# Key and value casts one step ahead, and a new order for the opening steps, in a retention and feed-forward kernel on one core

## The chip, the core and the metric

The kernel runs on one core of a Trainium2 chip. A core has a matrix engine (TensorE, PE in the profile; its weight loads are listed as PEld), a vector engine (VectorE, DVE), a scalar engine (ScalarE, ACT), GpSimd (POOL) and SyncE (SP), which here issues all transfers. Each engine works through a list of instructions of its own; semaphores tie the lists together. The metric is the time of one launch in microseconds, the median of several runs. Lower is better.

## What is computed

```python
gamma = 1.0 - 2.0 ** (-5.0 - np.arange(H, dtype=np.float32))
scale = 1.0 / np.sqrt(D)
for t in range(S):
    state = gamma[None, :, None, None] * state + np.einsum('bhd,bhe->bhde', k[:, :, t], v[:, :, t])
    y[:, :, t] = scale * np.einsum('bhd,bhde->bhe', q[:, :, t], state)
...
x = np.ascontiguousarray(attn_out.transpose(0, 2, 1, 3)).reshape(B * S, H * D)
...
a = x @ w1
b = x @ w2
h = a * b @ w3
return (h @ w_out).astype(np.float32)
```

Batch 4, 8 heads, 768 positions, head size 64; w1 and w2 are 512 x 1024, w3 is 1024 x 1024, w_out 1024 x 512. All inputs and the output (3072 x 512) are float32.

## The kernel before

w3 and w_out are multiplied first into one matrix (W3O), so each block of rows needs three products: with w1, with w2, and, after their elementwise product, with W3O. Operands are cast to 16 bits on the way in.

The recurrence is worked in chunks of 128 positions, two batch elements at a time: 6 chunks for 2 pairs of batch elements make 12 steps, m = 0 to 11. A chunk is split into two halves of 64 positions. For a step m the parts are:

- `load_k`, `load_v`, `load_q`: transfers from HBM into staging tiles (22 buffers of 512 KB, `wstage`), all issued by SP in the order of the calls. `load_q(n)` covers two chunks of one batch element, so two of them serve two steps.
- `q_cast`, `k_cast` (L269, L283): casts to 16 bits, on GpSimd or ScalarE; `v_cast` (L290): cast with the decay factors, on GpSimd.
- The transposes of queries and keys: in the opening on TensorE (`q_transposes`, `k_transposes`, L302 and L330, with copies back from PSUM by VectorE or ScalarE), later by transfers that SP issues (`q_dma` L313, `k_dma` L335).
- `scores` (L358) and their masking on VectorE (L365); `intra` (L380), the part of the output within a half; `kv` (L400), the new term of the state, with its backs on VectorE (L414, L417) and GpSimd (L418); `inter` (L431), the part of the output from the state; `outputs_back` (L440), which makes the rows x for the feed-forward part.
- The feed-forward part `Ffn(m)`: eight A units (four matmuls L460 into one of four psF banks, copied out by ScalarE, L469), eight B units (four matmuls L460, multiplied with A on VectorE, L475), and two output units (eight matmuls L485, scaled by ScalarE, L489, written out by SP, L490).

The order on each engine is the order of the calls in the source[...]. One call of `step(m)` does `inter` of step m-1, `scores` of step m, the two output units of step m-2, then the A and B units of step m-1 with `intra` and `kv` of step m in between. It also runs the preparation: keys, values and queries are loaded about three steps ahead and cast about two steps ahead (`k_cast(m + 2)` stands between the A units, `q_cast(m + 4)` at the end of GpSimd's list).

The opening is written out by hand: weights of W3O first, then the queries, keys and values of step 0, w1, keys and values 1, w2, and so on. The feed-forward part of step 0 goes by rows of w1 and w2 (`by_rows`, L570) so that each weight tile is used as it arrives; its W1 results are parked in two staging tiles (`hold`). `busy(n)` (L503) issues n matmuls on zeros. A few lines that set the order in the loop:

```python
if m > 2:
    q_dma(m + 3)
    load_k(m + 3)
    ffn[m - 2].o_unit(0)
    load_v(m + 3)
    ffn[m - 2].o_unit(1)
    load_q(m + 5)
...
elif m + 2 < NSTEP:
    k_cast(m + 2, (nc.scalar,))
    v_cast(m + 2, (nc.gpsimd, nc.gpsimd))
q_cast(m + 4, nc.gpsimd)
```

Of the kernel before, what the change touches and what calls it, by code (L numbers as in the profile page):

```python
# [18 lines left out]
def kernel(  # L19
# [11 lines left out]
    nc = tc.nc  # L31
# [5 lines left out]
    NSTEP = (B // 2) * NCH  # L37
# [4 lines left out]
    K_PE = 4  # L42
# [23 lines left out]
    def load_q(n):  # L66

        g, e = divmod(n, 2)
        if g >= NSTEP // 2:
            return  # L70
        bp, cp = divmod(g, NCH // 2)
        t = new_stage()
        dma_in(
            t[:, :].rearrange("p (h x) -> p h x", x=2 * D),
            q[bp * 2 + e, :, cp * 2 * C : (cp + 1) * 2 * C, :].rearrange("h (p t) d -> p h (t d)", t=2),
        )
        q_in[n] = t

    def load_k(m):
        load_kv(m, k_in, k)  # L80

    def load_v(m):
        load_kv(m, v_in, v)
# [41 lines left out]
    w3_st = {f: load_rows(moe_w3, f) for f in range(4, 8)}  # L125
    load_q(0)
    load_q(1)
    load_k(0)
    load_v(0)
    w1_st = [load_rows(moe_w1, d) for d in range(4)]  # L130
    load_k(1)
    load_v(1)
    w2_st = [load_rows(moe_w2, d) for d in range(4)]
    load_q(2)
    load_q(3)
    for m in range(2, 5):
        load_k(m)
        load_v(m)
        load_q(m + 2)

    Z = const.tile([128, 512], HP, name="zeros")
    nc.vector.memset(Z[:, :].bitcast(FP), 0.0)  # L142
# [42 lines left out]
    W1 = [wpool.tile([128, DFF], HP, name=f"w1_{i}") for i in range(4)]  # L185
# [6 lines left out]
    def cast_to(dst, src, on_dve):  # L192
        if on_dve:
            nc.vector.tensor_copy(dst, src)
        else:
            nc.scalar.copy(dst, src)  # L196
# [78 lines left out]
    def k_cast(m, engs):  # L275
        k16 = att.tile([128, 2, 512], HP, tag="k16", name="k16", bufs=3)
        k32 = k_in.pop(m)
        if len(engs) == 1:
            parts = [(k16[:, :, :].rearrange("p e x -> p (e x)"), k32[:, :, :].rearrange("p e x -> p (e x)"))]
        else:  # L280
            parts = [(k16[:, e, :], k32[:, e, :]) for e in range(2)]
        for eng, (dst, src) in zip(engs, parts):
            (nc.scalar.copy if eng is nc.scalar else eng.tensor_copy)(dst, src)  # L283
        k16s[m] = k16
# [37 lines left out]
    def k_transposes(m, tag, on_dve):  # L322
        k16, kT = k16s[m], new_kT(m)
        if tag:
            ps = bank(tag, [128, 2, NP, 128], HP, "psTk")
        else:
            ps = ps_f.tile([128, 2, NP, 128], HP, tag="psF", name="psTk")
        for e in range(2):
            for p in range(NP):
                nc.tensor.transpose(ps[:, e, p, :], k16[:, e, p * 128 : (p + 1) * 128], ident16[:, :])  # L330
        for e in range(2):
            cast_to(kT[:, e, :, :], ps[:, e, :, :], on_dve[e])
# [17 lines left out]
    def scores(m, engs=None):  # L350
        kT = kTs.pop(m)
        am = att.tile([128, 2, NP * 2, L], HP, tag="am", name="am")
        ps = [bank(f"X{r}", [128, NP * 2, L], FP, "psA") for r in range(2)]
        for e in range(2):
            for p in range(NP):
                for r in range(2):
                    for s in range(2):
                        nc.tensor.matmul(  # L358
                            ps[r][half(s), p * 2 + e, :], lhsT=kT[half(r), e, p, half(s)],
                            rhs=queries(m, e, p, s, r), start=True, stop=True,  # L360
                        )
        AMs[m] = am

        def back(r):
            nc.vector.tensor_tensor(  # L365
                am[:, r, :, :], ps[r][:, :, :],
                keep[:, :].unsqueeze(1).broadcast_to((128, NP * 2, L)), MULT,
            )

        return back  # L370
# [52 lines left out]
    def inter(m):  # L423
        ps = psYs[m]
        t = [Ts[m, s] for s in range(2)]
        first = t[0] is None
        for e in range(2):
            for p in range(NP):
                u = p * 2 + e
                for s, r in ((1, 0), (1, 1)) if first else ((1, 0), (0, 1), (0, 0), (1, 1)):  # L430
                    nc.tensor.matmul(  # L431
                        ps[s][half(r), u, :], lhsT=t[s][half(r), u * L : (u + 1) * L],
                        rhs=queries(m, e, p, s, r), start=False, stop=(e == 1 and p == NP - 1),
                    )
# [62 lines left out]
    def cast_w(W, st, d, on_dve):  # L497
        cast_to(W[d][:, :], st[d][:, :], on_dve)

    def busy(m, tag="Y0"):  # L500
        ps = bank(tag, [128, 512], FP, "psZ")
        for _ in range(m):
            nc.tensor.matmul(ps[:, :], lhsT=Z[:, 0:128], rhs=Z[:, 0:512], start=True, stop=True)  # L503
# [30 lines left out]
    k_transposes(0, "X0", (True, False))  # L534
    w3o_back()
    v_cast(0, (nc.gpsimd, nc.vector))
    nc.gpsimd.tensor_copy(W1[1][:, :], w1_st[1][:, :])
    cast_w(W1, w1_st, 0, False)
    backs = []

    def first_scores():
        backs.append(scores(0))

    w3o_back = w3_mm(7, first_scores)
    w3o_back()
    backs[0](0)
    backs[0](1)
    intra(0)
    backs.append(kv(0, True))
    busy(3, "X0")  # L550
    backs[1](0)
    inter(0)
    busy(3, "X1")
    outputs_back(0, 0)
    outputs_back(0, 1)
    backs[1](1)
    cast_w(W1, w1_st, 2, False)
    cast_w(W1, w1_st, 3, False)

    ffn = [Ffn(m) for m in range(NSTEP)]  # L560
    f0, f1 = ffn[0], ffn[1]
# [3 lines left out]
    def four_banks():  # L565
        return [ps_f.tile([128, 2, TB], FP, tag="psF", name="psF")[:, :, :] for _ in range(4)]

    def by_rows(W, ps, d, blocks=range(8)):
        for f in blocks:
            nc.tensor.matmul(  # L570
                ps[f // 2][:, f % 2, :], lhsT=W[d][:, f * 128 : (f + 1) * 128],
                rhs=f0.x(d), start=(d == 0 and f % 2 == 0), stop=(d == 3 and f % 2 == 1),
            )

    k_cast(1, (nc.gpsimd, nc.scalar))
    ps = four_banks()
    by_rows(W1, ps, 0)
    by_rows(W1, ps, 1)
    by_rows(W1, ps, 2)
    k_transposes(1, "Y0", (True, False))  # L580
    by_rows(W1, ps, 3, range(4))
    pa = [hold[i // 2][:, i % 2 * 512 : i % 2 * 512 + 512].rearrange("p (a n) -> p a n", a=2) for i in range(4)]
    am_back = scores(1)
    by_rows(W1, ps, 3, range(4, 8))
    for i in range(4):
        cast_to(pa[i], ps[i], False)
    am_back(0)
    am_back(1)
    v_cast(1, (nc.gpsimd, nc.gpsimd))
    nc.gpsimd.tensor_copy(W2[0][:, :], w2_st[0][:, :])  # L590
    ps = four_banks()
    cast_w(W2, w2_st, 1, False)
    intra(1)
    kv_back = kv(1)
    kv_back(0, nc.vector)
    by_rows(W2, ps, 0)
    inter(1)
    outputs_back(1, 1)
    outputs_back(1, 0)
    cast_w(W2, w2_st, 2, False)  # L600
    nc.gpsimd.tensor_copy(W2[3][:, 512:1024], w2_st[3][:, 512:1024])
    q_cast(2, nc.gpsimd)
    kv_back(1)
    by_rows(W2, ps, 1)
    nc.scalar.copy(W2[3][:, 0:512], w2_st[3][:, 0:512])
    by_rows(W2, ps, 2)
    f1.a_unit(0, "X0")
    by_rows(W2, ps, 3)
    for i in range(4):
        nc.vector.tensor_tensor(f0.HT[:, 2 * i : 2 * i + 2, :], pa[i], ps[i], MULT)  # L610
    q_cast(3, nc.gpsimd)
    for f, tag in ((1, "Y1"), (2, "Y0"), (3, "X1"), (4, "X0"), (5, "Y1"), (6, "Y0"), (7, "X1")):
        f1.a_unit(f, tag)
    k_cast(2, (nc.gpsimd, nc.scalar))
    q_transposes(2, "X0", True)
    f0.o_unit(0)
# [1 line left out]
    q_transposes(3, "Y0", True)  # L618
    k_transposes(2, "Y1", (True, False))
    f0.o_unit(1)  # L620
    k_cast(3, (nc.scalar,))

    def step(m):

        if m > 2:
            inter(m - 1)
            outputs_back(m - 1, 0)
            outputs_back(m - 1, 1)
        if m >= NSTEP:
            return  # L630
        am_back = scores(m)
        am_back(0)
        am_back(1)
        if K_PE <= m < NSTEP - 1:
            k_dma(m + 1)
        if m > 2:
            q_dma(m + 3)
            load_k(m + 3)
            ffn[m - 2].o_unit(0)
            load_v(m + 3)  # L640
            ffn[m - 2].o_unit(1)
            load_q(m + 5)
        for f in range(2):
            ffn[m - 1].ab(f)
        intra(m)
        kv_back = kv(m)
        kv_back(0)
        ffn[m - 1].ab(2)
        ffn[m - 1].ab(3)
        kv_back(1)  # L650
        if m == 2:
            k_transposes(3, None, (True, False))
            q_cast(4, nc.gpsimd)
            q_dma(4)
            v_cast(3, (nc.gpsimd, nc.gpsimd))
            k_cast(4, (nc.scalar,))
            k_dma(4)
            q_cast(5, nc.scalar)
            q_dma(5)
            v_cast(4, (nc.gpsimd, nc.gpsimd))  # L660
            load_k(5)
            load_v(5)
            load_q(7)
        elif m + 2 < NSTEP:
            k_cast(m + 2, (nc.scalar,))
            v_cast(m + 2, (nc.gpsimd, nc.gpsimd))
        q_cast(m + 4, nc.gpsimd)
        for f in range(4, 8):
            ffn[m - 1].ab(f)

    for m in range(2, NSTEP):
        step(m)
    step(NSTEP)
    last = ffn[NSTEP - 1]
# [36 lines left out]
```

## Time and profile before

| | |
|---|---|
| median of 7 runs | 200.07 us (199.41 to 203.5) |
| the profiled execution | 200.9 us |
| its span, first to last instruction | 199.2 us |
| mean granted TensorE clock | 0.972 |
| read from HBM, written to it | 29.36 MB, 6.29 MB |
| share of 16 DMA engines in use by SP's queue | 84.1% of the span |
| TensorE's longest wait | 6.5 us, L460 for ScalarE's L469 |
| ScalarE's waits for keys (L283) | 14.8 us in 6 waits, the longest 6.8 |

Four transfers of the list, from issue to landing (medians): weights 512 KB 6.5 us, queries 512 KB 6.2 us, half of a step's keys 256 KB 4.7 us, an output block 256 KB 4.3 us; a transpose of queries takes 3.8 us and one of keys 5.5 us.

How to read it: the page cuts the span into 40 slices of 4.98 us and gives for each engine the busy share of each slice in tenths; PEclk is the clock that TensorE was granted in each slice, DMA the mean busy share of the 16 DMA engines. The chain of waits follows the work that ended last back to what released it; each of its lines has a start, a length and what it is. In a timeline, square brackets give the idle time of an engine before an instruction and what ended it. The trace also records when each transfer landed, and the granted clock with its times.

### The profile page before, as it was taken

To read this page: it belongs to the slowest core of one execution; us is meant where nothing else is said; L and a number is where in the kernel's file an instruction comes from. 1 tells how busy PE (TensorE), PEld (TensorE's weight loads), DVE (VectorE), ACT (ScalarE), POOL (GpSimd) and SP (SyncE) were. 2 spreads that over 40 slices of the span, in tenths; PEclk is the share of its full clock that TensorE was granted. 3 is DMA by queue.
4 is the path that set the end of the run, shared out by engine and by line. 5 is a ranking of instruction groups with operands and counts; after the bars stand their busy time and mean duration, and the time that the engine had idled before them with its cause. 6 is when DMAs were issued, how large, how long until landed. Compare 5 with 4: busy or idle time off the path is not lost.

```text
span 199.2 us, 6231 instructions
## 1 busy us (share of the span) xinstructions
PE 182.4 (92%) x2651; PEld 127.9 (64%) x2651; DVE 97.4 (49%) x187; ACT 84.6 (42%) x163; POOL 66.3 (33%) x94
## 2 busy tenths in 40 slices
PE   7899998779998970999999999999999999999993
PEld 2445655558666560658678585886858768686772
DVE  1226356338368331346735566364665746555240
ACT  5478547554541712225235252443515334232422
POOL 6200233435718515603807016280532605020000
PEclk9999999969999999599999999999999999999999
DMA  6999999999999999999999999996952220110202
GB/s 213 362 390 381 253 266 345 264 367 223 232 218 229 238 185 233 237 276 191 273 227 252 219 241 276 211 226 136 274 57 100 56 105 3 55 54 3 105 0 105
DMA packets 87338, 40.23 MB, mean 202 GB/s; under 512 B 67728, under 2 KB 82320, under 8 KB 87312
## 3 DMA queue, kind: packets, MB, share of 16 engines
q1 hardware_dynamic: 87312, 39.85, 84.1%
q8 instruction: 20, 0.33, 0.7%
q14 instruction: 6, 0.05, 0.1%
HBM read 29.36 MB, written 6.29 MB: 179 GB/s over the span
## 4 chain that ended last, share of the span: by engine, by line
PE 63%; DMA 19%; SPq 12%; issue 2%; POOL 2%; ACT 1%; ACTq 0%; POOLq 0%
PE psF L460 35%; PE psO L485 18%; SPq L60 11%; DMA stg<-in_k_dram 9%; DMA stg<-in_moe_w_out_dram 4%; PE psY L431 3%; DMA stg<-in_moe_w_dram 3%; DMA stg<-in_v_dram 3%; PE psF L570 2%; PE psY L380 2%; PE psA L358 1%; PE psK L400 1%; POOL v L290 1%; SPq L313 1%; POOL w L590 1%
## 5 line engine op out<-in xcount | busy, mean ns | idle before, releaser
L460 PE MATMUL psF<-xt,w 128*128 128x256 f16 x672 | 79.3, 276 | 7.4 <-ACT pa L469 6.5
L460 PEld LDWEIGHTS <-w 128*128 128x128 f16 x704 | 68.7, 99 | 19.0 <-issue 7.9
L475 DVE TENSOR_TENSOR ht<-pa,psF 128x256 f16<-128x256 f32 x88 | 36.6, 421 | 55.0 <-ACT pa L469 29.1
L418 POOL TENSOR_TENSOR t<-s,GS 128x512 f16<-128x512 f32 x19 | 24.1, 1269 | 69.8 <-DVE s L417 68.9
L469 ACT COPY pa<-psF 128x256 f32<-128x256 f32 x80 | 29.7, 372 | 35.8 <-PE psF L460 35.8
L485 PE MATMUL psO<-w3o,ht 128*128 128x512 f16 (+2 forms) x200 | 44.1, 373 | 0.0
L485 PEld LDWEIGHTS <-ht 128*128 128x128 f16 x200 | 18.6, 98 | 20.0 <-issue 0.5
L489 ACT ACTIVATE osb<-psO 128x512 f32<-128x512 f32 (+2 forms) x25 | 14.4, 580 | 40.1 <-PE psO L485 40.1
L290 POOL TENSOR_TENSOR v<-stg,VS 128x512 f16<-128x512 f32 x23 | 23.6, 1045 | 9.4 <-DMA stg<-in_v_dram 9.4
L417 DVE TENSOR_TENSOR s<-psK,t 128x512 f32<-128x512 f32 x20 | 13.8, 688 | 8.3 <-POOL t L418 4.7
L269 POOL CAST q<-stg 128x1024 f16<-128x1024 f32 x10 | 10.4, 1039 | 22.3 <-DMA stg<-in_q_dram 17.1
L440 DVE TENSOR_TENSOR xt<-psY,YS 128x512 f16<-128x512 f32 x24 | 16.1, 722 | 3.4 <-PE psY L431 2.5
L283 ACT CAST k<-stg 128x1024 f16<-128x1024 f32 (+1 forms) x12 | 11.3, 940 | 14.8 <-DMA stg<-in_k_dram 14.8
L365 DVE TENSOR_TENSOR am<-psA,keep 128x512 f16<-128x512 f32 x24 | 15.3, 677 | 2.6 <-PE psA L358 2.6
L215 DVE COPY w3t<-psW 128x1024 f16<-128x1024 f16 x8 | 5.4, 689 | 12.0 <-PE psW L223 9.5
L196 ACT CAST w3h<-stg 128x1024 f16<-128x1024 f32 x8 | 8.3, 1044 | 3.6 <-DMA stg<-in_moe_w_dram 3.2
L570 PE MATMUL psF<-xt,w 128*128 128x256 f16 x64 | 8.8, 291 | 0.7 <-POOL w L590 0.6
L431 PEld LDWEIGHTS <-t 64*64 64x64 f16 x352 | 7.2, 117 | 3.3 <-issue 2.5
L503 PE MATMUL psZ<-zeros 128*128 128x512 f16 x19 | 7.6, 553 | 1.3 <-DVE zeros L142 1.3
L244 PE MATMUL psW<-wo,w3t 128*128 128x512 f16 x32 | 8.6, 409 | 0.0
L431 PE MATMUL psY<-qT,t 64*64 64x64 f16 x352 | 8.5, 202 | 0.1
L257 PE MATMUL psW<-wo,w3t 128*128 128x512 f16 x32 | 8.1, 380 | 0.4 <-DVE w3t L215 0.4
(58 smaller groups left out, 115.3 us busy)
## 6 DMA issues: line engine op xcount, KB each, us to landing
stg<-in_moe_w_dram SPq DMA_DIRECT2D x16, 512.0 KB, 6.5
stg<-in_q_dram SPq DMA_DIRECT2D x12, 512.0 KB, 6.2
stg<-in_k_dram SPq DMA_DIRECT2D x24, 256.0 KB, 4.7
stg<-in_v_dram SPq DMA_DIRECT2D x24, 256.0 KB, 5.1
out_dram<-osb SPq DMA_DIRECT2D x23, 256.0 KB, 4.3
stg<-in_moe_w_out_dram SPq DMA_DIRECT2D x4, 512.0 KB, 7.9
out_dram<-osb SPq DMA_DIRECT2D x1, 160.0 KB, 1.8
qT<-q SPq DMA_TRANSPOSE x8, 3.8
```

The costliest lines, as they stand in the source:

```text
L60: nc.sync.dma_start(dst, src)
L290: eng.tensor_tensor(v16[:, e, :].rearrange("j (h d) -> j h d", d=D), v32[:, e, :].rearrange("j (h d) -> j h d", d=D), VS[:, :].unsqueeze(2 ...
L365: nc.vector.tensor_tensor(am[:, r, :, :], ps[r][:, :, :], keep[:, :].unsqueeze(1).broadcast_to((128, NP * 2, L)), MULT,)
L417: nc.vector.tensor_tensor(s32[:, :], kvs, Ts[m, s][:, :], ADD)
L418: eng.tensor_tensor(t16[:, :], s32[:, :], gs, MULT)
L431: nc.tensor.matmul(ps[s][half(r), u, :], lhsT=t[s][half(r), u * L : (u + 1) * L], rhs=queries(m, e, p, s, r), start=False, stop=(e == 1 an ...
L440: nc.vector.tensor_tensor(XT[m][:, :, s, :].rearrange("p u (i t) -> p u t i", t=2), psYs[m][s][:, :, :].rearrange(order, t=2), YS[:, :, :] ...
L460: nc.tensor.matmul(ps[:, :], lhsT=W[d][:, f * 128 : (f + 1) * 128], rhs=self.x(d), start=(d == 0), stop=(d == 3),)
L469: nc.scalar.copy(self.pa[f][:, :], ps[:, :])
L475: nc.vector.tensor_tensor(self.HT[:, f, :], self.pa.pop(f)[:, :], ps[:, :], MULT)
L485: nc.tensor.matmul(psO[:, :], lhsT=self.HT[:, f, e * 128 : (e + 1) * 128], rhs=W3O[f][:, cs], start=(f == 0), stop=(f == 7),)
L489: nc.scalar.activation(osb[:, cs], psO[:, :], AF.Copy, scale=final_scale)
```

## The change

Casts of keys and values move from two steps ahead to one, and the loads from three steps to two. In the opening, keys and values 1 are loaded ahead of w1, cast and transposed behind step 0, and the whole of step 1's recurrence comes before the rows of w1; the A units of step 1 are spread between the rows of w2. Step 2 gets an order of its own (`step2`), in which queries 4 and 5 and keys 3 are cast. In the loop, the key cast and its transpose stand between the two output units, queries are cast two at a time in even steps and transposed two at a time in the following odd step.

```diff
-    load_k(0)
-    load_v(0)
+    for m in range(2):
+        load_k(m)
+        load_v(m)
     w1_st = [load_rows(moe_w1, d) for d in range(4)]
-    load_k(1)
-    load_v(1)
     w2_st = [load_rows(moe_w2, d) for d in range(4)]
     load_q(2)
     load_q(3)
     for m in range(2, 5):
         load_k(m)
         load_v(m)
-        load_q(m + 2)
+        load_q(m + 2) if m < 4 else None
...
     v_cast(0, (nc.gpsimd, nc.vector))
-    nc.gpsimd.tensor_copy(W1[1][:, :], w1_st[1][:, :])
-    cast_w(W1, w1_st, 0, False)
+    k_cast(1, (nc.gpsimd, nc.scalar))
     backs = []
...
     w3o_back = w3_mm(7, first_scores)
-    w3o_back()
     backs[0](0)
     backs[0](1)
     intra(0)
     backs.append(kv(0, True))
-    busy(3, "X0")
     backs[1](0)
+    k_transposes(1, "X0", (False, False))
+    w3o_back()
     inter(0)
-    busy(3, "X1")
     outputs_back(0, 0)
     outputs_back(0, 1)
     backs[1](1)
-    cast_w(W1, w1_st, 2, False)
-    cast_w(W1, w1_st, 3, False)
+    v_cast(1, (nc.gpsimd, nc.gpsimd))
+    nc.gpsimd.tensor_copy(W1[1][:, :], w1_st[1][:, :])
+    for d in (0, 2, 3):
+        cast_w(W1, w1_st, d, False)
...
-    k_cast(1, (nc.gpsimd, nc.scalar))
-    ps = four_banks()
-    by_rows(W1, ps, 0)
-    by_rows(W1, ps, 1)
-    by_rows(W1, ps, 2)
-    k_transposes(1, "Y0", (True, False))
-    by_rows(W1, ps, 3, range(4))
     pa = [hold[i // 2][:, i % 2 * 512 : i % 2 * 512 + 512].rearrange("p (a n) -> p a n", a=2) for i in range(4)]
+    busy(2, "X1")
     am_back = scores(1)
-    by_rows(W1, ps, 3, range(4, 8))
-    for i in range(4):
-        cast_to(pa[i], ps[i], False)
     am_back(0)
     am_back(1)
-    v_cast(1, (nc.gpsimd, nc.gpsimd))
-    nc.gpsimd.tensor_copy(W2[0][:, :], w2_st[0][:, :])
-    ps = four_banks()
-    cast_w(W2, w2_st, 1, False)
     intra(1)
     kv_back = kv(1)
     kv_back(0, nc.vector)
-    by_rows(W2, ps, 0)
+    ps = four_banks()
+    by_rows(W1, ps, 0)
     inter(1)
     outputs_back(1, 1)
     outputs_back(1, 0)
+    by_rows(W1, ps, 1)
+    kv_back(1)
+    nc.gpsimd.tensor_copy(W2[0][:, :], w2_st[0][:, :])
+    by_rows(W1, ps, 2)
+    by_rows(W1, ps, 3)
+    for i in range(4):
+        cast_to(pa[i], ps[i], i % 2 == 1)
+    cast_w(W2, w2_st, 1, False)
+    for f, tag in ((0, "X0"), (1, "Y1"), (2, "Y0"), (3, "X1")):
+        f1.a_unit(f, tag)
+    ps = four_banks()
+    by_rows(W2, ps, 0)
     cast_w(W2, w2_st, 2, False)
+    for f, tag in ((4, "X0"), (5, "Y1"), (6, "Y0"), (7, "X1")):
+        f1.a_unit(f, tag)
+    by_rows(W2, ps, 1)
+    nc.scalar.copy(W2[3][:, 0:512], w2_st[3][:, 0:512])
     nc.gpsimd.tensor_copy(W2[3][:, 512:1024], w2_st[3][:, 512:1024])
     q_cast(2, nc.gpsimd)
-    kv_back(1)
-    by_rows(W2, ps, 1)
-    nc.scalar.copy(W2[3][:, 0:512], w2_st[3][:, 0:512])
     by_rows(W2, ps, 2)
-    f1.a_unit(0, "X0")
     by_rows(W2, ps, 3)
...
-    for f, tag in ((1, "Y1"), (2, "Y0"), (3, "X1"), (4, "X0"), (5, "Y1"), (6, "Y0"), (7, "X1")):
-        f1.a_unit(f, tag)
...
-    k_cast(3, (nc.scalar,))
+
+    def step2():
+        am_back = scores(2)
+        am_back(0)
+        am_back(1)
+        q_cast(4, nc.scalar)
+        k_cast(3, (nc.scalar,))
+        q_dma(4)
+        for f in range(4):
+            f1.ab(f)
+        intra(2)
+        kv_back = kv(2)
+        kv_back(0)
+        f1.ab(4)
+        f1.ab(5)
+        kv_back(1)
+        v_cast(3, (nc.gpsimd, nc.gpsimd))
+        f1.ab(6)
+        k_transposes(3, None, (True, False))
+        q_cast(5, nc.scalar)
+        q_dma(5)
+        f1.ab(7)
...
-        if K_PE <= m < NSTEP - 1:
+        if m > 3 and m % 2:
+            q_dma(m + 1)
+            q_dma(m + 2)
+        ffn[m - 2].o_unit(0)
+        if m + 1 < NSTEP:
+            k_cast(m + 1, (nc.scalar,))
             k_dma(m + 1)
-        if m > 2:
-            q_dma(m + 3)
-            load_k(m + 3)
-            ffn[m - 2].o_unit(0)
-            load_v(m + 3)
-            ffn[m - 2].o_unit(1)
-            load_q(m + 5)
+        ffn[m - 2].o_unit(1)
+        load_q(m + 3) if m % 2 == 0 else None
+        load_k(m + 2)
+        load_v(m + 2)
+        load_q(m + 3) if m % 2 else None
...
-        if m == 2:
-            k_transposes(3, None, (True, False))
-            q_cast(4, nc.gpsimd)
-            q_dma(4)
-            v_cast(3, (nc.gpsimd, nc.gpsimd))
-            k_cast(4, (nc.scalar,))
-            k_dma(4)
-            q_cast(5, nc.scalar)
-            q_dma(5)
-            v_cast(4, (nc.gpsimd, nc.gpsimd))
-            load_k(5)
-            load_v(5)
-            load_q(7)
-        elif m + 2 < NSTEP:
-            k_cast(m + 2, (nc.scalar,))
-            v_cast(m + 2, (nc.gpsimd, nc.gpsimd))
-        q_cast(m + 4, nc.gpsimd)
+        if m + 1 < NSTEP:
+            v_cast(m + 1, (nc.gpsimd, nc.gpsimd))
+        if m % 2 == 0:
+            q_cast(m + 2, nc.gpsimd)
+            q_cast(m + 3, nc.gpsimd)
         for f in range(4, 8):
             ffn[m - 1].ab(f)
 
-    for m in range(2, NSTEP):
+    step2()
+    for m in range(3, NSTEP):
         step(m)
     step(NSTEP)
```

More of the change, by code (lines that the diff above doesn't have):

```diff
@@ L620 @@
     f0.o_unit(1)
-    k_cast(3, (nc.scalar,))
+    def step2():
[19 more added lines that the diff above has]
+        f1.ab(7)
     def step(m):
-        if m > 2:
-            inter(m - 1)
-            outputs_back(m - 1, 0)
-            outputs_back(m - 1, 1)
+        inter(m - 1)
+        outputs_back(m - 1, 0)
+        outputs_back(m - 1, 1)
         if m >= NSTEP:
@@ L633, in step @@
         am_back(1)
-        if K_PE <= m < NSTEP - 1:
-            k_dma(m + 1)
-        if m > 2:
-            q_dma(m + 3)
-            load_k(m + 3)
-            ffn[m - 2].o_unit(0)
-            load_v(m + 3)
-            ffn[m - 2].o_unit(1)
-            load_q(m + 5)
+        if m > 3 and m % 2:
[4 more added lines that the diff above has]
+            k_cast(m + 1, (nc.scalar,))
+            k_dma(m + 1)
+        ffn[m - 2].o_unit(1)
[3 more added lines that the diff above has]
+        load_q(m + 3) if m % 2 else None
         for f in range(2):
```

## The prediction

> **What bounds the kernel now.** I read the page first (engine shares, the 40 slices), then the waits by engine, then the chain of waits in order of time, then the timeline around each gap of TensorE.
>
> ```profile
> PE 182.4 (92%) x2651; PEld 127.9 (64%) x2651; DVE 97.4 (49%) x187; ACT 84.6 (42%) x163; POOL 66.3 (33%) x94
> PE   7899998779998970999999999999999999999993
> PEclk9999999969999999599999999999999999999999
> DMA  6999999999999999999999999996952220110202
> ```
>
> TensorE is busy 182.4 of 199.2 us, so only 16.8 us could be won without removing matmuls, and nearly all of it lies before slice 18 (90 us). From there to 182 us the PE digits are 9: each step takes 12.17 us (the chain has the output blocks L485 at 97.47 and 109.64) and the transfers are hidden. Up to about 135 us the DMA digits are 9: work before that is paced by what has landed. The one large hole is slice 15 (a 0), and the clock falls to 5 in slice 17.
>
> ```profile
> 73.59 0.57 SPq L60
> 74.16 0.05 issue
> 74.22 4.25 DMA stg<-in_k_dram
> 78.47 0.02 issue
> 78.49 0.04 ACTq L283
> ...
> 79.52 0.38 ACT pa L469
> 79.89 0.04 issue
> 79.94 3.57 PE psF L460 x16
> 83.51 0.88 PE psY L431 x16
> ...
> 84.93 3.92 PE psO L485 x16
> 88.85 1.75 PE psF L460 x16
> ```
>
> ```profile
> 78.57 1.04 ACT L283 CAST k<-stg 128x1024 f16<-128x1024 f32 x1 [6.84 <-DMA stg<-in_k_dram]
> 79.94 3.57 PE L460 MATMUL psF<-xt,w 128*128 128x256 f16 x16 [6.49 <-ACT pa L469]
> ```
>
> ```profile
> 73.40:80.00 6.60, 0.11 (x2) 0.06 (x1) 0.77 (x2) 1.43 (x3) 3.76 (x4) 0.91 1.19 229
> 80.00:85.60 5.60, 5.60 (x82) 3.79 (x82) 2.58 (x6) 0.91 (x3) 2.88 (x3) 0.50 1.28 240
> 85.60:97.80 12.20, 12.20 (x209) 9.12 (x208) 6.69 (x14) 4.92 (x11) 4.68 (x5) 1.00 1.18 245
> ```
>
> In the last fence (stretches: length, busy PE, PEld, DVE, ACT, POOL, granted clock, DMA share, GB/s) the reader sees the hole and its echo. In step 3 ScalarE stands at the cast of keys 5 (L283), issued by SP only at 73.59 and landed at 78.47; the psF evictions L469 queue behind it, the four psF banks stay full, and TensorE waits 6.49 us. Then it runs at clock 0.50 until 85.6: 16 matmuls take 3.57 us instead of 1.75.
>
> **What the Trainium skill says.** "TensorE: Matmul & The Clock Gate", section "What's actually happening": an idle activity window of about 3.4 us halves the array's clock, a busy one restores it. The trace agrees: 0.50 right after the 6.49 us gap. The table at the head of that page calls ScalarE, VectorE and GpSimd queues strict FIFO; the fence above shows it, L469 not passing L283. "DMA: Bandwidth & Descriptors", section "Issuing engines are not separate DMA queues": all transfers share 16 engines. Here all come from SP, and the trace's landings follow issue order: the order of the list decides arrival.
>
> **The change, part by part.** All sums are against the profiled execution: 200.9 us, 199.2 of it span; the median of seven runs is 200.07.
>
> *Keys one step ahead.* Step 3 now casts keys 4 instead of 5. Keys 4 landed at 65.48 and keep their place in the list, so the wait for keys 5 leaves step 3. Removed: 6.49 us of stall; 3.57 - 1.75 = 1.82 for 16 matmuls at half clock; and step 4's own half-clock share, (96.58 - 83.51) - 12.17 = 0.90. Sum 9.2 us. Late next: in step 4, which would start at 83.51 - 6.49 - 1.82 = 75.2, two things. Its scores need the transposed keys 4. Before, SP issued that transpose at 69.61 and it landed at 74.86, behind queries 6, two output blocks and one query transpose; now it stands behind two query transposes and three output blocks. From successive landings queries 6 cost 1.7 us of DMA, a transpose 0.9, an output block 0.65: 0.9 + 0.65 replaces 1.7, so again about 74.9. Second, the cast of keys 5, at step start + 0.9 (L431, L358) + 1.78 (first output block) + 0.60 (eviction L489) = 78.5. Ahead of keys 5 the list has two output blocks more (1.3) and queries 6 less (1.7): landing at 78.5 again, or a little earlier. Nor does a small delay count: TensorE has banks for two output blocks and two L460 units, so keys may land up to about 4.2 us into the step (79.4). I take 0 for both; upper bound 1.5 us.
>
> *The cast between the two output evictions.* In steps 3 to 10 the 1.05 us cast sits between the L489s instead of among the L469s. First eviction ends at start + 3.3, cast at 4.3, second output block at 4.5, eviction 5.1, first L469 5.5; the bank that the fourth L460 unit needs (5.8) is free at 5.1. Cost 0, hidden behind L485, provided that keys are there by 4.2. They are issued a step earlier, after the second output's write: at latest some 10 us into the step (two query transposes, one key transpose, two outputs at 1.2 to 1.7 us each on SP), plus 4 to 5 us landing, is 2 to 3 us into the next. Slack 1 to 2 us in odd steps, about 5 in even ones. Per two steps the DMA moves what it moved before (three steps from 92.81 to 125.87 at full load by landings, 11.0 us each), less than 12.17.
>
> *Two query casts on GpSimd every even step* instead of one each step: 2 x 1.04 after the value casts, ending about 2.9 us into the odd step, where SP needs them. GpSimd's next job (L418) comes 7.5 us into a step. Cost 0; if queries land late SP's list waits and the slack above shrinks.
>
> *Opening order.* Keys and values 1 move ahead of w1: by the landings before (values 0 at 28.56; then 1.1 to 1.2 per half) keys 1 are in by 30.8, values 1 by about 33; w1 still ends at 39.4, as before. Chain: kv(0) ends 31.3; key transposes to 32.1; inter(0) to 32.6; two L440 to 34.0; L417 to 34.7; L418 on GpSimd to 36.0; the two value casts, queued behind it, at 37.0 and 38.0. So intra(1) ends at 38.4, kv(1) at 38.8, against 41.2 before: 2.4 us earlier, but all four W1 rows (32 x 0.11 = 3.5 us) now come after it, where before they filled the waits. TensorE is nearly idle from 33.7 to 37, so the window from 37.9 should run at half clock: the first row costs 1.75, inter(1) 0.85. Then rows 1 to 3 end at 44.1, four L460 units at 45.9, first W2 row 46.8, the other four units 48.5, rows 1 and 2 50.3, row 3 (waiting for ScalarE's last weight half) 51.5. Before, the same work was over at 50.8. Both then wait for the products L610; scores(2) at about 56.5 instead of 55.65: a loss of 0.85. The removed and added fillers (3 + 3 against 2) lie in waits and count nothing. A second half-clock window would add 1.7; a clock that stays full would take off 1.3.
>
> *Step 2.* Same eight B units; products of units 4 and 5 come ahead of the second state update, so the key copy on VectorE ends at 63.4, scores(3) start at 63.5, output blocks at 63.9 (63.21 before). In step 3 ScalarE has casts of queries 5 (63.4 to 64.4), eviction 66.3, keys 4 to 67.3, eviction 68.05: no wait for psF, whereas before a 0.4 us wait and the order of evictions held the second pair of units to 68.12. intra(3) starts at 69.25, before 69.21. So the opening's loss is used up here and the net of both is 0.
>
> Sum: 0 - 9.2, so 191.7 for an execution like the profiled one and 190.9 from the median; for the unproven zeros (key transpose at 74.9 against a need at 75.3) I add 0.3: 191.2.
>
> **The rivals.**
> A, as worked out: 191.2, range 189.5 to 193.
>
> B, the opening loses more: value casts later by a DMA hiccup (successive landings before show jumps of about 1.2 us) or a second half-clock window, 1.7 + 1.2: 194.1. For: the thin work at 34 to 38 us. Against: the full clock returned after 3.4 us at 44.7 before, with similar work.
>
> C, the stall moves: keys 5 or transposed keys 4 arrive 1.5 to 3 us too late in step 4 and half the echo comes back, 3 + 1.5: 195.7. For: the DMA is at 9 there. Against: it has no more bytes ahead of keys 5 than before.
>
> D, slower: the steps become bound by a loop through SP. A key cast releases the key transpose, then the second output's write, then the next key load, whose landing releases the next cast. Low: 1.05 + 1.24 (transpose issue, at 142.47) + 0.4 + 0.4 + 0.6 + 3.7 = 7.4 us. High, with the longest issues seen under load: 1.05 + 3.86 (at 87.12) + 1.64 + 0.7 + 1.04 + 4.9 = 13.2, and 14 in an odd step with SP held by the queries' casts. It decides when it passes 12.17 + 9.2 / 8 = 13.3 on average over eight steps. At 13.7 it gives 190.9 + 8 x 1.5 = 203. For: loads are one step less ahead. Against: the long issues belong to a full DMA queue; a step that waits drains it.
>
> E, nothing gained: a mixture of B and D that eats 9 us: 200.
>
> **How the numbers follow.** A 0.66, B 0.13, C 0.10, D 0.08, E 0.03. Faster by over 0.5%: A + B + C = 0.89; within 0.5% (about what a measurement of this kernel can tell from no change): 0.03; slower: 0.08. The time is that of A. The range takes A's own bounds, B, and the lower part of C: 189.3 to 195.5, leaving out D, E and the top of C.
>
> **What would show it.** Right: no TensorE gap above 1 us between 65 and 85 us, no 0.5 in the clock digits there, step 4 starting near 75, steps still 12.2 us; intra(1) near 38, scores(2) near 56.5. Wrong: a wait of L469 or L489 behind the key cast in odd steps (D), scores waiting for kT near 75 (C), clock 0.5 beyond 41.3 us (B).

## The result, and the profile after

| | before | after |
|---|---|---|
| median | 200.75 us (31 runs) | 192.25 us (12 runs, 191.41 to 192.96) |
| profiled execution, span | 200.9, 199.2 us | 191.6, 189.9 us |
| mean granted TensorE clock in it | 0.972 | 0.991 |

The ratio is 0.9583, with a 95% interval of 0.9553 to 0.9612: 8.4 us less. The forecast was 191.2, range 189.3 to 195.5. More runs of the kernel before have moved its median from 200.07 to 200.75. Medians count every execution, while ratios and their intervals leave out those over 1.5% above the fastest of their kernel, so that the two can differ, by up to 1 us below.

The page of the changed kernel, the lines that answer to those shown of before (lines of the same code stand one number lower, L459 for L460):

```profile
PE 178.6 (94%) x2647; PEld 126.5 (67%) x2647; DVE 97.5 (51%) x188; ACT 85.1 (45%) x163; POOL 64.9 (34%) x93
PE   7799997299999799999999999999999999999993
PEclk9999999969999999999999999999999999999999
DMA  5999999999999999999999999999999950110202
```

The 0 in TensorE's digits and the 5 in the clock's are gone (slices 15 and 16 of before, counted from 0; the prediction put the 5 in slice 17). One thin place is left, slices 7 and 8 (33 to 43 us), with the only low clock digit. The DMA digits now stay at 9 to slice 31, where before they fell after slice 26: the same bytes are spread over more of the run. Stretches of the changed kernel (length; busy PE, PEld, DVE, ACT, POOL; clock; DMA share; GB/s):

```profile
34.00:37.60 3.60, 0.32 (x16) 0.21 (x16) 1.44 (x3) 1.04 (x1) 3.27 (x4) 1.00 0.95 366
37.60:41.00 3.40, 3.36 (x84) 2.52 (x86) 1.38 (x2) 2.09 (x2) 0.97 (x1) 0.50 1.01 410
...
65.00:85.00 20.00, 20.00 (x328) 14.90 (x327) 10.52 (x22) 8.97 (x19) 6.21 (x6) 1.00 1.16 217
```

From 65 to 85 us TensorE is busy all 20 us; before it stood still for 6.5 of them. The price is in the first two lines: hardly any matmul from 34.0 to 37.6 us, then half clock. TensorE's timeline at both places:

```profile
36.64 0.32 PE L379 MATMUL psY<-am,v 64*64 64x64 f16 x16 [2.70 <-POOL v L289]
37.64 0.43 PE L379 MATMUL psY<-am,v 64*64 64x64 f16 x16 [0.68 <-POOL v L289]
...
69.71 5.41 PE L459 MATMUL psF<-xt,w 128*128 128x256 f16 x48
75.05 0.63 PE L430 MATMUL psY<-qT,t 64*64 64x64 f16 x28
```

In the hole of the opening, TensorE waits for the casts of values 1 on GpSimd. Step 3's twelve groups of four matmuls (x48) run through without a stop, and step 4 begins at 75.05 instead of 83.44.

### The profile page after: what moved, and what is told of

The parts are those of the page before. It is cut to its first block, busy times and chain, and to the rows that moved or that the text cites. A ratio compares the mean times of both kernels' runs of the same rounds, so it can differ in the third digit from the quotient of the medians.

```text
span 189.9 us, 6226 instructions
## 1 busy us (share of the span) xinstructions
PE 178.6 (94%) x2647; PEld 126.5 (67%) x2647; DVE 97.5 (51%) x188; ACT 85.1 (45%) x163; POOL 64.9 (34%) x93
## 4 chain that ended last, share of the span: by engine, by line
PE 78%; SPq 8%; DMA 7%; issue 3%; POOL 2%; ACT 0%; DVE 0%; DVEq 0%; ACTq 0%; POOLq 0%
PE psF L459 39%; PE psO L484 23%; SPq L60 8%; DMA stg<-in_moe_w_out_dram 5%; PE psF L569 4%; PE psY L430 3%; DMA stg<-in_k_dram 2%; PE psY L379 2%; PE psG L459 2%; PE psA L357 2%; PE psK L399 2%; POOL v L289 1%; POOL t L417 1%; PE psTq L301 0%; PE psTk L329 0%
## 5 line engine op out<-in xcount | busy, mean ns | idle before, releaser
L459 PE MATMUL psF<-xt,w 128*128 128x256 f16 x672 | 77.1, 273 | 0.0
L459 PEld LDWEIGHTS <-w 128*128 128x128 f16 x704 | 68.0, 98 | 10.4 <-issue 0.2
L474 DVE TENSOR_TENSOR ht<-pa,psF 128x256 f16<-128x256 f32 x88 | 36.6, 420 | 50.3 <-ACT pa L468 26.4
L417 POOL TENSOR_TENSOR t<-s,GS 128x512 f16<-128x512 f32 x19 | 24.1, 1266 | 77.3 <-DVE s L416 75.6
L484 PE MATMUL psO<-w3o,ht 128*128 128x512 f16 (+2 forms) x200 | 44.1, 371 | 0.0
L488 ACT ACTIVATE osb<-psO 128x512 f32<-128x512 f32 (+2 forms) x25 | 14.5, 579 | 33.5 <-PE psO L484 30.6
L268 POOL CAST q<-stg 128x1024 f16<-128x1024 f32 x9 | 9.2, 1039 | 17.6 <-DMA stg<-in_q_dram 17.6
L214 DVE COPY w3t<-psW 128x1024 f16<-128x1024 f16 x8 | 5.5, 690 | 11.8 <-PE psW L222 9.4
L379 PE MATMUL psY<-am,v 64*64 64x64 f16 x384 | 5.8, 197 | 3.9 <-POOL v L289 3.4
L379 PEld LDWEIGHTS <-v 64*64 64x64 f16 x384 | 4.4, 110 | 6.7 <-POOL v L289 3.6
L243 PE MATMUL psW<-wo,w3t 128*128 128x512 f16 x32 | 8.5, 406 | 0.0
L569 PE MATMUL psF<-xt,w 128*128 128x256 f16 x64 | 8.5, 291 | 0.0
```

Source lines behind the costliest of these rows:

```text
L417: eng.tensor_tensor(t16[:, :], s32[:, :], gs, MULT)
L459: nc.tensor.matmul(ps[:, :], lhsT=W[d][:, f * 128 : (f + 1) * 128], rhs=self.x(d), start=(d == 0), stop=(d == 3),)
L474: nc.vector.tensor_tensor(self.HT[:, f, :], self.pa.pop(f)[:, :], ps[:, :], MULT)
L484: nc.tensor.matmul(psO[:, :], lhsT=self.HT[:, f, e * 128 : (e + 1) * 128], rhs=W3O[f][:, cs], start=(f == 0), stop=(f == 7),)
L488: nc.scalar.activation(osb[:, cs], psO[:, :], AF.Copy, scale=final_scale)
L569: nc.tensor.matmul(ps[f // 2][:, f % 2, :], lhsT=W[d][:, f * 128 : (f + 1) * 128], rhs=f0.x(d), start=(d == 0 and f % 2 == 0), stop=(d == ...
```

## The experiments

The first four runs split the change, the next four price what the split left open, the last four narrow down or repeat. Ratios are against the kernel before on the same chip.

**1. Old opening, new loop.** The load order and opening of the kernel before, with `step2` and the new `step`; only the load of queries 6 goes with the new loop.

```diff
 # of the changed kernel, put back as before
-    for m in range(2):
-        load_k(m)
-        load_v(m)
+    load_k(0)
+    load_v(0)
     w1_st = [load_rows(moe_w1, d) for d in range(4)]
+    load_k(1)
+    load_v(1)
...
 # and the opening from k_transposes(0) to o_unit(1) as before
```

> Opening and load order of the kernel before, with the new order of step 2 and the new loop. Theory (the loop carries the whole gain, the new opening costs about 0.5 us, scores(2) at 55.65 instead of 56.18): 191.5 to 192.8 us, no gap of TensorE over 1 us between 65 and 85 us. Rival (the new opening brings a part of the gain, by loading keys and values 1 early): 193.5 us or more.

Measured 191.82 us, ratio 0.9571 (0.9520 to 0.9623). As the theory had it: against the 0.9583 of the whole change, the new opening brings nothing that this can tell from zero, in either direction.

**2. New opening, old loop.** The converse.

```diff
+    k_cast(3, (nc.scalar,))
...
-    step2()
-    for m in range(3, NSTEP):
+    for m in range(2, NSTEP):
         step(m)   # step as before
```

> New opening and load order, with step 2 and the loop of the kernel before. Theory (the stall at the cast of keys 5 belongs to the loop): 200 to 202 us, with the 6 to 7 us gap before an L459 group in step 3 and a half clock after it. Rival (the opening brings a part): under 199 us.

Measured 200.56, ratio 1.0005 (0.9982 to 1.0028). The gap in front of an L459 group is there; TensorE's waits in the profiled execution (202.3 us, the longest of the twenty) have it as us in total, times, longest:

```profile
PE psF L459 <- ACT pa L468: 7.7, 1, 7.7
```

So the gain belongs to the loop, with its `step2`.

**3. The cast alone.** In the kernel before, the casts of keys and values and the transpose behind the key cast move to their new places; the loads still run three steps ahead.

```diff
-        if K_PE <= m < NSTEP - 1:
-            k_dma(m + 1)
...
             ffn[m - 2].o_unit(0)
+            if m + 1 < NSTEP:
+                k_cast(m + 1, (nc.scalar,))
+                k_dma(m + 1)
...
-        elif m + 2 < NSTEP:
-            k_cast(m + 2, (nc.scalar,))
-            v_cast(m + 2, (nc.gpsimd, nc.gpsimd))
+        elif m + 1 < NSTEP:
+            v_cast(m + 1, (nc.gpsimd, nc.gpsimd))
```

> The kernel before, with the key cast and its transpose put between the output units and keys and values cast one step ahead, but loads still three steps ahead and queries as before. Theory (what counts is what SP issues ahead of the transposed keys 4): the loads of keys 5 and 6, values 5 and queries 7 now stand ahead of that transpose, it lands near 83 us instead of 75, and the wait moves to the scores of step 4: 198 to 202 us. Rival (the place of the cast on ScalarE alone carries the gain): 191 to 193 us.

Measured 205.58, ratio 1.0274 (1.0213 to 1.0335): slower than before, and above the expected 198 to 202. TensorE's timeline of this kernel:

```profile
77.38 2.11 PE L460 MATMUL psF<-xt,w 128*128 128x256 f16 x12 [4.54 <-DVE ht L475]
...
86.93 0.64 PE L358 MATMUL psA<-qT,kT 64*64 64x64 f16 x32 [6.45 <-DMA kT<-k]
```

and SP's list:

```profile
71.91 1.69 SPq L60 DMA_DIRECT2D stg<-in_k_dram  x2
73.64 2.39 SPq L60 DMA_DIRECT2D stg<-in_v_dram  x2
76.07 1.32 SPq L60 DMA_DIRECT2D stg<-in_q_dram  x1
...
80.00 1.61 SPq L60 DMA_DIRECT2D stg<-in_k_dram  x2
...
82.80 1.30 SPq L335 DMA_TRANSPOSE kT<-k  x1
```

The wait for transposed keys 4 is the expected one: the loads above the last line are for later steps, and SP issues them first, so the transpose goes out at 82.80 (at 70.08 in the changed kernel) and lands at 86.9 (I had said 83). The other wait, 4.54 us for the products L475, was not expected. Its cause can be read in the profile of the kernel before, where the wait for keys 5 covers it. GpSimd's timeline there:

```profile
73.95 1.04 POOL L269 CAST q<-stg 128x1024 f16<-128x1024 f32 x1 [4.26 <-DMA qT<-q]
74.95 1.26 POOL L418 TENSOR_TENSOR t<-s,GS 128x512 f16<-128x512 f32 x1
```

and VectorE's:

```profile
76.24 0.69 DVE L417 TENSOR_TENSOR s<-psK,t 128x512 f32<-128x512 f32 x1 [4.01 <-POOL t L418]
```

`q16` has two buffers, so the cast of queries 6, the last entry of step 2 on GpSimd, waits until the transpose of queries 4 has read one of them. Behind it stands step 3's L418, behind that VectorE's L417, and behind that the products that free psF. An estimate from these lines: with keys 5 in place, VectorE would still have held TensorE until about 77.3 us (76.24, plus 0.69 for L417 and 0.42 for a product), and in run 3 TensorE goes on at 77.38.

**4. The gap filled.** The kernel before, with 26 matmuls on zeros where TensorE stands still.

```diff
         for f in range(4, 8):
+            if m == 3 and f == 6:
+                busy(26, "X0")
             ffn[m - 1].ab(f)
```

> The kernel before with 26 extra matmuls on zeros in step 3 ahead of the seventh A unit, where TensorE stands still for 6.5 us; nothing else is changed. Theory (2.7 us of the gain are the half clock after the gap): the gap's end stays near 80 us, the next 16 matmuls take 1.75 us instead of 3.57, and the time is 198.0 us (197.5 to 198.6). Rival (the slow stretch after the gap is DMA or something else, and fillers only occupy): 200.7 us or more.

TensorE's timeline of this kernel, and one of its stretches (clock 1.00, where the kernel before has 0.50):

```profile
73.15 5.77 PE L503 MATMUL psZ<-zeros 128*128 128x512 f16 x26
79.89 1.93 PE L460 MATMUL psF<-xt,w 128*128 128x256 f16 x16 [0.96 <-ACT pa L469]
81.74 0.63 PE L431 MATMUL psY<-qT,t 64*64 64x64 f16 x28
```

```profile
80.00:85.60 5.60, 5.60 (x94) 3.59 (x93) 3.97 (x8) 1.45 (x4) 2.81 (x3) 1.00 1.29 239
```

The gap's end has not moved (79.89), the 16 matmuls behind it take 1.93 us in the timeline instead of 3.57, and step 4 starts 1.7 us sooner: half clock after the gap is a real cost, and work that computes nothing takes it away. But the median is 199.47, ratio 0.9950 (0.9928 to 0.9971): 1.0 us, not 2.7, and the time lies above the 197.5 to 198.6 of the theory. The profiled execution of the kernel before had a mean clock of 0.972; 29 of the 39 beside this run have 0.981 or more, so the profiled one had most likely drawn a longer stretch at half clock than is usual. Whether that is all of the difference was not tested; a term taken from the one execution was too large for the median.

**5. Queries 6 early.** The changed kernel with the load and the cast of queries 6 put back to where they were.

```diff
-        load_q(m + 2) if m < 4 else None
+        load_q(m + 2)
...
         q_dma(5)
+        q_cast(6, nc.gpsimd)
         f1.ab(7)
...
-        load_q(m + 3) if m % 2 else None
+        load_q(m + 3) if m % 2 and m > 3 else None
...
-            q_cast(m + 2, nc.gpsimd)
+            if m > 4:
+                q_cast(m + 2, nc.gpsimd)
```

> The changed kernel with one thing put back: queries 6 are loaded at the end of the opening list and cast on GpSimd at the end of step 2, as before. Theory (in the kernel before a second wait stood behind the one for keys 5: GpSimd sat at the cast of queries 6 until the transpose of queries 4 had landed, and its state update L418 and the products behind it were late): GpSimd waits for a qT landing near 72 us, the products of step 3 come about 3 us later than now, TensorE waits 1 to 2.5 us in step 3, and the time rises by 1.5 to 3 us, to 193.7 to 195.3. Rival (the keys' cast was the only wait, and the query casts cost nothing wherever they stand): 191.8 to 192.8.

The profiled execution took 193.48 us, just under the expected 193.7 to 195.3, and shows the chain as described; GpSimd:

```profile
72.16 1.04 POOL L268 CAST q<-stg 128x1024 f16<-128x1024 f32 x1 [6.57 <-PE psF L459]
73.16 1.26 POOL L417 TENSOR_TENSOR t<-s,GS 128x512 f16<-128x512 f32 x1
```

TensorE:

```profile
75.53 1.47 PE L459 MATMUL psF<-xt,w 128*128 128x256 f16 x12 [1.66 <-DVE ht L474]
```

(The releaser named in GpSimd's bracket is a guess of the profile: the cast starts at 72.16, right after the transpose of queries 4 has landed at 71.95.) The other three executions took 197.6, 198.2 and 198.5, so that the median of the four, 197.89, is above the expected range; there is no ratio for this kernel. A second profiled execution (run 12) drew the short time again:

> The kernel with queries 6 early once more, for a second profile. Three of its four executions took 4 to 5 us longer than the profiled one. Theory (with step 4 later by 2 us the loads shift against SP's list and a key load comes too late in a later step, as with the added loads): L459 waits for L488 behind a key cast, or scores wait for kT, after step 4. Rival (the opening differs from execution to execution): the loss lies before 60 us. If it falls into the short group again, 193.5, nothing is learned.

193.6 us, with a wait of 1.3 us for L474. So the two profiled executions bear out that the second wait exists, with 1.3 and 1.7 us of TensorE; what the three longer ones lost besides is not known.

**6 and 7. One and two more loads a step.** The changed kernel with further loads of 256 KB, whose data nothing reads.

```diff
         load_q(m + 3) if m % 2 else None
+        if m < 10:
+            spare = new_stage()[:, :].rearrange("p (e x) -> p e x", e=2)
+            for e in range(1):        # 2 in the second kernel
+                dma_in(
+                    spare[:, e, :].rearrange("p (h d) -> p h d", d=D),
+                    k[e, :, 0:C, :].rearrange("h i d -> i h d"),
+                )
```

> The changed kernel with one more load of 256 KB in each of steps 3 to 9, at the end of SP's list of the step, into a staging tile that nothing reads. Theory A (the DMA needs 11.0 of the 12.17 us of a step and has 1.2 us to spare): no more than 1 us slower, under 193.3. Theory B (the steps already use all the DMA has, and the loop only just holds): each extra load of 1.05 us counts in full from some step on, 4 to 7.5 us slower, 196 to 199.8.

> The same with two loads of 256 KB a step. Theory A (1.2 us to spare): 13.1 against 12.17 us in up to 7 steps, 5 to 7 us slower, 197 to 199.5. Theory B (nothing to spare): 7 x 2.1 = 12 to 15 us slower, 204 to 207.

One load: 194.74, ratio 0.9732 (0.9687 to 0.9777), 2.5 us above the changed kernel. Two: 204.06, ratio 1.0177 (1.0127 to 1.0227), 11.8 us above, slower than the kernel before. One load lies between the two theories; two loads lie at the lower end of theory B, nothing to spare. ScalarE's key casts with one load more:

```profile
116.64 1.04 ACT L282 CAST k<-stg 128x1024 f16<-128x1024 f32 x1 [1.82 <-DMA stg<-in_k_dram]
...
142.39 1.04 ACT L282 CAST k<-stg 128x1024 f16<-128x1024 f32 x1 [1.64 <-DMA stg<-in_k_dram]
```

and the same in the changed kernel:

```profile
115.30 1.04 ACT L282 CAST k<-stg 128x1024 f16<-128x1024 f32 x1 [0.55 <-DMA stg<-in_k_dram]
```

With one load more, TensorE waits 1.0 us in step 7 and 0.8 us in step 9 for the output eviction L488 behind such a cast; with two, 7.2 us in four waits for L488 and 2.9 us in three for kT, and a window of half clock (95.1 to 98.5) at the longest of them. These are the waits that rival D names. That its loop through SP sets the pace is not shown: with two loads more the DMA share is 1.02 to 1.34 in every stretch of 12 us from 75 to 171, so that a DMA with no room left explains them as well, and the waiting steps did not drain its queue as the prediction thought. In the changed kernel the limit is just not felt: keys 8 land at 115.23, which is 3.64 us into step 7 (start 111.59), and the psF banks last to about 4.2.

**8. Values first.** The changed kernel, one line moved in the opening.

```diff
-    backs[1](1)
     v_cast(1, (nc.gpsimd, nc.gpsimd))
+    backs[1](1)
```

> The changed kernel with the casts of values 1 put ahead of the state update L417 of step 0 on GpSimd; nothing else. Theory (the opening's hole at 34 to 38 us comes from that order, but what follows is paced by landings of queries 2 and 3, keys 2 to 5): intra(1) over by 36 instead of 38.1 us, half-clock windows fewer, but only 0.3 to 1.2 us of it reach the end: 191.0 to 191.9. Rival (an opening hole counts in full): 2.4 us, 189.8.

Measured 190.99, ratio 0.9534 (0.9491 to 0.9577). TensorE's timeline of it:

```profile
35.12 0.19 PE L379 MATMUL psY<-am,v 64*64 64x64 f16 x1 [0.96 <-DVE am L364]
35.72 0.44 PE L379 MATMUL psY<-am,v 64*64 64x64 f16 x31 [0.41 <-DVE am L364]
...
73.53 0.63 PE L430 MATMUL psY<-qT,t 64*64 64x64 f16 x28
```

Of the 3.4 us of waits at intra(1) 1.4 are left, the clock stays full in this execution, and step 4 starts at 73.53: the 1.5 us won reach the loop. The time is at the lower edge of the theory's range; the rival's 2.4 us did not come.

**9. The keys' part alone.** The kernel before with keys and values as in the new loop, and queries as before.

```diff
-        if K_PE <= m < NSTEP - 1:
-            k_dma(m + 1)
         if m > 2:
+            ffn[m - 2].o_unit(0)
+            if m + 1 < NSTEP:
+                k_cast(m + 1, (nc.scalar,))
+                k_dma(m + 1)
+            ffn[m - 2].o_unit(1)
+            load_k(m + 2)
+            load_v(m + 2)
             q_dma(m + 3)
-            load_k(m + 3)
-            ffn[m - 2].o_unit(0)
-            load_v(m + 3)
-            ffn[m - 2].o_unit(1)
             load_q(m + 5)
...
```

> The kernel before with the keys' and values' part of the new loop alone: cast one step ahead between the output units, loaded two steps ahead, key transpose ahead of the later loads; queries 6 and 7 are loaded, cast and transposed as before (cast of queries 6 at the end of step 2 on GpSimd, queries 7 loaded ahead of the transposed keys 4). Theory (two waits stood behind each other in step 3, and the queries' part removes the second): TensorE now waits about 3 to 4 us in step 3 for the products behind GpSimd, up to 1.5 us for kT in step 4, and half the gain is lost: 194.5 to 198. Rival (the keys' part carries all): 191.5 to 192.8.

Measured 197.44, ratio 0.9878 (0.9845 to 0.9911): 2.4 us by the ratio, 3.2 by the medians. The changed kernel beside it (run 10) gains 7.5 and 8.5, so about 5 us come only with the rest. GpSimd and TensorE of this kernel:

```profile
75.21 1.04 POOL L269 CAST q<-stg 128x1024 f16<-128x1024 f32 x1 [7.76 <-DMA qT<-q]
76.21 1.26 POOL L418 TENSOR_TENSOR t<-s,GS 128x512 f16<-128x512 f32 x1
```

```profile
78.58 2.72 PE L460 MATMUL psF<-xt,w 128*128 128x256 f16 x12 [3.17 <-DVE ht L475]
81.22 0.65 PE L431 MATMUL psY<-qT,t 64*64 64x64 f16 x28
```

With keys 5 out of the way, TensorE stops 3.17 us for the products behind the query cast, as the theory had it; the clock halves again for 3.4 us, and no wait for kT is left. (This execution reached step 3 about 2 us later than the one of before, 65.30 against 63.21 for the first output block, so its starts are not to be set against those one by one.) What is missing here is the queries' part and `step2` together; how much of the 5 us belongs to either was not separated.

**10 and 11. The changed kernel and values first, side by side.**

> The changed kernel as it is, to stand beside the next run on the same chip: 191.4 to 193.0.

> The casts of values 1 ahead of the state update of step 0 on GpSimd, a second time, beside the changed kernel on the same chip. Theory (the opening's hole reaches the end by more than half, since kT and keys 5 still land in time when step 4 starts 1.5 us earlier): 1.0 to 1.5 us below the changed kernel. Rival (the first measurement of it was luck of the clock): no difference.

192.12, as expected, ratio 0.9626 (0.9581 to 0.9671), against 191.39, ratio 0.9567 (0.9528 to 0.9606): 0.7 us less by the medians, 1.2 by the ratios, where 1.0 to 1.5 was expected, and the intervals overlap. With run 8 (1.3 us less by the medians) the direction is the same twice, but the size is not settled. In the profiled execution of run 11 the half clock is back (37.7 to 41.1 us), so values first do not always hold the clock. By its medians it is the fastest version tried.

## Why the prediction was right, and where it was not

*The stall of step 3.* Right in size, with one of two causes missing. The step "the wait for keys 5 leaves step 3. Removed: 6.49 us of stall" holds for the whole change: step 4 starts at 75.05, predicted 75.2. But it does not follow from the keys' part, to which I put it down. Two waits stood one behind the other. The queries' part was priced at "Cost 0", and no gain was looked for in it or in `step2`; run 9, which has neither, lacks about 5 us. The profile had the second wait, 4.01 us of VectorE for GpSimd's L418; I read only the wait that ended last. That the sum came out right was in part luck: the change happened to remove the second wait too.

*The echo.* Mechanism right (run 4), size too large for the median: 1.82 + 0.90 in the profiled execution, 1.0 in the medians. Between the two profiled executions the sum of 9.2 us does hold: their spans differ by 9.3. The changed one, though, is one of the four of twelve with a clock of 0.991, and the medians differ by 8.4. The echo is enough to account for that 0.8 us; that it is the only reason was not tested. The limit of 16.8 us for the whole gain was not a limit either: TensorE's busy time itself fell by 3.8 us, from 182.4 to 178.6, in part because the 16 matmuls behind the gap counted 3.57 us in it instead of 1.75.

*What is late next in step 4.* Right. The scores of step 4 ran at 75.49 with no wait shown for kT; keys 5 landed at 78.54 (78.5) and the cast began at 78.64 (78.5). Run 3 shows what SP's order was worth: the same cast with three steps of loads ahead of the transpose costs 5.1 us more than the kernel before, and about 8 more than run 9, from which it differs in SP's list alone.

*The room in the loop.* "Cost 0" for the cast between the evictions held, but "slack 1 to 2 us in odd steps, about 5 in even ones" was too generous and put it in the wrong place. The keys loaded in even steps stand behind a query load and come last: 3.64 us into step 7 against 4.2, about 0.6 us. Runs 6 and 7 point the same way: loads worth 7 x 1.05 = 7.4 us cost 2.5, and twice as much, 14.7, cost 11.8, so an estimate of 0.4 to 0.7 us a step could be absorbed, not 1.2.

*The opening.* intra(1) ended at 38.1 (38.4), kv(1) at 38.5 (38.8), half clock ran from 37.6 to 41.0, rows of w1 to 44.0 (44.1), scores(2) at 56.18 (56.5): a loss of 0.53 instead of 0.85. A second half-clock window was a rival at 1.7 us; it seems to be the usual case. Four of the twelve executions have a mean clock of 0.991 and spans of 189.7 to 190.1; the other eight have 0.980 to 0.982 and 190.2 to 191.3: about 0.9 us. The profiled execution of run 10, the same kernel, shows the longer form: half clock from 38.1 to 45.0.

*Step 2.* scores(3) began at 62.7 (63.5), output blocks at 63.64 (63.9), intra(3) at 68.94 (69.25, and 69.14 before in TensorE's timeline): the opening's loss is made up here, as forecast.

## What to carry to other kernels

A wait that ends last can cover another that ends just before it. Before pricing its removal, ask for every engine's idle time in the same stretch, and take the second-latest end as the new limit. A preparation moved later is worth only what the issuing queue lets through: in run 3 the cast moved and the loads ahead of its transpose did not, and the kernel lost 5.1 us. And a term read from one execution's clock should be checked against the mean clock of the other runs.

## What was not expected of the hardware

How long TensorE stays at half clock differs between executions of the same kernel: 3.4 us in the profiled execution of the changed kernel, 6.8 in that of run 10, and the two groups of executions are about 0.9 us of 190 apart. The stretch ahead of it need not be empty: in the 3.4 us before the clock halved TensorE was busy for 0.3 us in the changed kernel, 1.4 in run 11 and 2.2 in the opening of the kernel before, while run 8, with 1.8 of 3.6 us, kept the full clock. How much work is enough is not settled here. And 26 matmuls on zeros made a kernel 0.5% faster: in the profiled execution the clock stayed full through the gap and behind it.
